# Float64 weights decoded by a shifted upper word plus a remainder, with the list of operations written anew, in a delta-rule and gated-MLP kernel

## The chip, the cores and the metric

One NeuronCore of one Trainium2 chip runs the whole program. The metric is the device time of one execution in microseconds (us); several runs are made and the median counts.

## What is computed

Four batches of eight heads run a delta rule over 768 steps with a 48 by 48 state, and the result `x` (4 x 768 x 384) goes through a gated MLP with a spatial gate:

```python
y[:, :, t] = einsum('bhd,bhde->bhe', q[:, :, t], state)
v_old = einsum('bhde,bhd->bhe', state, kt)              # kt: normalised key
state = state + bt * einsum('bhd,bhe->bhde', kt, vt - v_old)
...
h = maximum(x @ w_in, 0.0)                              # w_in 384 x 1024
u, v = h[..., :512], h[..., 512:]
v_n = (v - mean(v)) / sqrt(var(v) + 1e-06)
v_s = einsum('ts,bsd->btd', w_spatial, v_n) + b_spatial[None, :, None]
out = (u * v_s) @ w_out                                 # w_out 512 x 384
```

`w_in` and `w_out` are scaled by `1.0 / np.sqrt(...)` and so reach the kernel as float64; all else is float32. [...] 

## The kernel before

The recurrence is worked in chunks of 64 steps: 24 steps `s` (two halves of the batch, 12 chunks each), each for 16 batch-head pairs at once. Four steps form a group `g` (six groups). `prep(g)` loads `k`, forms the key products on TensorE (`kk`), copies them to a tile `xt` (L391), transposes the 32x32 blocks into `la` (L569, VectorE), normalises by the key lengths (L577 to L591), inverts the triangular blocks, and transposes the result back into `xt` (L638). Groups 0 and 1 have mode "w": there the inversion is 16 wide and runs on VectorE in PSUM (`lanes16`, L623 to L628), and `widen16` completes it with TensorE matmuls (tiles `bbc`, `gi`: L702, L718, L720). Groups 2 to 5 have mode "p": a 32-wide inversion on GpSimd (`lanes`, L608 and L613). After this `widen(s)` (tiles `tn`, `pi`), `kqt(s)` and `step(s)` carry the state from chunk to chunk.

Every second step gives a tile of 2 x 128 rows of `x` (`convert`, tiles `xh` and `xl`) to the MLP: `mlp_v` (matmuls with `win` as the 512-wide moving operand), `norm_v`, `mlp_u` (256 columns), and, when a batch half is complete, `gate` with the spatial matmuls (`wsph`, `wspl`) and the output (`wout`). The first MLP matmul needs all six tiles of `w_in` decoded; `weights()` decodes them, 128 x 512 each, and then four tiles of `w_out`, 128 x 384 each.

`load_f64` decodes one tile. With `w1` the upper and `w0` the lower word: L450 (VectorE) takes the exponent field out of `w1`; L452, L453 and L454 (ScalarE) clamp it and turn it into the exponent of a float32; L455 (ScalarE) turns `w0` into a fraction; L456 (VectorE) adds the sign; L458 (VectorE) and L459 (ScalarE) turn the mantissa bits of `w1` into a fraction; L460 adds the two fractions and L461 multiplies by the power of two (VectorE or GpSimd). `split_w` then rounds to the high part (L440, ScalarE) and subtracts for the low part (L441, VectorE or GpSimd). That is six steps on ScalarE, three on VectorE, and three that a table gives to VectorE or GpSimd.

What sets the order: `Plan.add` records every operation with its reads, writes and pools; `emit` then issues them in the order of a table of numbers, `ORDER` (two letters an operation), and a second table, `PICK`, names the engine where there is a choice. Each engine runs its instructions in that order and waits where an input isn't ready. The pair of letters that stands for no operation (`Qq`) makes `emit` put in a filler: two matmuls of 128 x 256 on the mask tile `mpos` into a free PSUM bank, whose result nobody reads. All loads and stores are issued from SyncE (L410), all matmuls from L517 (`mm`).

Of the kernel before, what the change touches and what calls it, by code (L numbers as in the profile page):

```python
# [32 lines left out]
NRAW = 7  # L33
NFULL = 6
# [8 lines left out]
    "2/1T132:2;2<Qq5g4f5i5n3p3q3y8x4N3r5j3u3v3$3!2>3(3%3#2?2@3&2[2]2^2_2{2|2}2~2,3031325l3s3x3c8l1U1f5o1s141g5m1G4Q5p5s1t"
    "5r5u1H4O4m333t4S4g34Qq354R364T3738391u3w3z4h3)3*4i5t4U5v4V4j4k1hQq1v3+4W2=3A4l5w5y5z5x5!5#5$5%5&3B5(3C3D3E3F3G424344"
    "3<454X4Z463-3.3/4Y4a4n4p3:4d4c4y4e4b4o5)4q3H4r4z3=4s4t4u4#3;1y3I4w5Q5*4x4$47491z4)1!Qq4(4*5+5-5.5/1#5:4!5;5<5=5>5?5@"
    "4&5[4%5]5^5_5{5K1$5L5|3>3?3@8m8n3[485}5~5,5M6o6p5V5N60614A8o5P621%5R4+631&6n645O3]6g6566673^4B5S6h5W685T4v5U1(Qq6i69"
    "1)8p8u4C6j4D6A4E8r6k6q6z6B6C6%6D1*8q6l5X5Y6r6m6E4F4G1+6FQq6&Qq6G4-6H5Z6s6!4H6t6#8s8t6u6x6y1-8v6v6w6I6J6K6L6M7i1.6N6O"
# [1068 lines left out]
```

## Time and profile before

| | us |
|---|---|
| median of 3 runs | 487.97 (487.59 to 488.6) |
| the profiled execution | 483.41 |
| its span in the trace | 481.7 |
| PE busy | 426.6 |
| DVE busy | 247.9 |
| ACT busy | 253.1 |
| POOL busy | 216.4 |

PE is TensorE's matmul stream, PEld its weight load, DVE VectorE, ACT ScalarE, POOL GpSimd, SP SyncE, which issues the DMAs. The span is the time from the first to the last recorded instruction, 1.7 us less than the profiled execution's own time. The profile comes from one execution, 4.6 us faster than the median. "issue" in the trace is time in which an engine waited for nothing that the profile shows. A tile's number is left out in the trace's names (`ut` for any of the six `ut` buffers), and a tile that lies in another's memory has that one's name (`wspl`, `xt` and `la` stand for different tensors early and late in the program).

### The profile page before, as it was taken

How to read it: one execution, taken by the hardware profiler on the slowest of the kernel's cores; microseconds unless marked ns; L12 is line 12 of the kernel's file. 1: busy time of each engine (PE TensorE's matmuls, PEld its weight loads, DVE VectorE, ACT ScalarE, POOL GpSimd, SP SyncE). 2: the span in 40 equal slices, each digit the busy share in tenths (PEclk: the TensorE clock that was granted, in tenths of full speed). 3: DMA queues.
4: the chain of work that ended last, by engine and by line, in shares of the span. 5: the costliest groups of instructions: out<-in, count | busy, mean ns of one | idle time of the engine just before them, and what ended most of it. 6: DMA issues, size and time to landing. Idle time of an engine off the chain costs nothing.

```text
span 481.7 us, 21693 instructions
## 1 busy us (share of the span) xinstructions
PE 426.6 (89%) x9722; PEld 380.7 (79%) x9722; DVE 247.9 (51%) x550; ACT 253.1 (53%) x592; POOL 216.4 (45%) x357
## 2 busy tenths in 40 slices
PE   2437888777989899998999999999899999999996
PEld 2336666665877787876988989999799899999996
DVE  2798895544765658846707345252645132441212
ACT  3788674346576869776227633415625484431113
POOL 3105547883489832389944668840001400122310
PEclk9555579885999999999999999999999999999999
DMA  8632153140425455452130341101420100001012
GB/s 266 250 99 81 58 155 103 50 141 4 150 60 178 135 170 198 135 151 86 57 106 6 99 137 36 56 1 35 145 81 14 59 0 18 1 1 49 3 65 99
DMA packets 26108, 42.65 MB, mean 89 GB/s; under 512 B 4512, under 2 KB 14880, under 8 KB 26016
## 3 DMA queue, kind: packets, MB, share of 16 engines
q1 hardware_dynamic: 26016, 41.27, 27.2%
q8 instruction: 76, 1.25, 1.1%
q14 instruction: 16, 0.13, 0.1%
HBM read 35.36 MB, written 4.72 MB: 83 GB/s over the span
## 4 chain that ended last, share of the span: by engine, by line
PE 78%; DVE 6%; issue 6%; ACT 6%; DMA 3%; SPq 1%; DVEq 0%; ACTq 0%
PE ps L517 78%; DMA ke<-in_k_t 2%; ACT xt L391 1%; DVE ps L626 1%; DVE prod L623 1%; SPq L410 1%; DMA bn<-in_bun 1%; ACT gt L890 1%; DVE pt L750 1%; ACT w L803 0%; ACT ut L453 0%; ACT ut L454 0%; ACT ut L452 0%; DVE wspl L587 0%; ACT vr L880 0%
## 5 line engine op out<-in xcount | busy, mean ns | idle before, releaser
L517 PE MATMUL ps<-wsph,vf 128*128 128x256 f32 x528 | 107.4, 286 | 0.0
L517 PEld LDWEIGHTS ps<-wsph,vf 128*128 128x128 f32 x528 | 86.7, 191 | 1.3
L613 POOL TENSOR_TENSOR wl<-wl,prod 128x60 f32<-128x60 f32 (+7 forms) x120 | 74.1, 617 | 9.3
L517 PE MATMUL ps<-wspl,vf 128*128 128x256 f32 x264 | 74.6, 283 | 0.0
L608 POOL TENSOR_TENSOR prod<-wl,la 128x60 f32<-128x60 f32 (+7 forms) x120 | 67.8, 565 | 10.2 <-DVE ps L626 1.1
L973 DVE TENSOR_TENSOR gt<-ps,bbc 128x512 f32<-128x512 f32 x24 | 16.6, 691 | 68.8 <-PE ps L517 68.7
L517 PEld LDWEIGHTS ps<-wspl,vf 128*128 128x128 f32 x264 | 50.4, 191 | 0.3
L517 PE MATMUL ps<-wout_h,g 128*128 128x384 f32 x128 | 35.3, 341 | 0.0
L994 ACT COPY ob<-ps 128x384 f32<-128x384 f32 x24 | 11.2, 479 | 42.6 <-PE ps L517 40.6
L391 ACT COPY xt<-xt 32x128 f32<-32x128 f32 (+1 forms) x91 | 31.7, 349 | 2.1
L391 ACT COPY xt<-ps 128x512 f32<-128x512 f32 (+1 forms) x37 | 17.7, 481 | 27.6 <-PE ps L517 27.6
L750 DVE TENSOR_TENSOR pt<-ps,mpos 128x512 f32<-128x512 f32 (+1 forms) x29 | 16.7, 593 | 28.7 <-PE ps L517 25.0
L517 PE MATMUL ps<-bn 64*64 64x64 f32 (+2 forms) x896 | 20.4, 241 | 11.1 <-DMA bn<-in_bun 5.0
L517 PEld LDWEIGHTS ps<-bn 64*64 64x64 f32 (+1 forms) x896 | 16.9, 145 | 15.3 <-issue 4.6
L517 PE MATMUL ps<-ke 64*64 64x64 f32 (+2 forms) x768 | 18.9, 257 | 9.0 <-issue 4.8
L517 PEld LDWEIGHTS ps<-ke 64*64 64x64 f32 (+1 forms) x768 | 16.0, 160 | 13.4 <-issue 7.6
L803 ACT COPY w<-ps 128x384 f32<-128x384 f32 x24 | 11.5, 477 | 27.0 <-PE ps L517 26.9
L732 POOL TENSOR_TENSOR bn<-bn,nn 128x384 f32<-128x384 f32 x11 | 9.1, 835 | 36.4 <-DVE nn L600 15.9
L938 ACT ACTIVATE ut<-ps 128x256 f32<-128x256 f32 x48 | 17.9, 383 | 12.5 <-PE ps L517 12.4
L517 PEld LDWEIGHTS ps<-wout_h,g 128*128 128x128 f32 x128 | 23.2, 188 | 0.7
L517 PE MATMUL ps<-wout_l,g 128*128 128x384 f32 x64 | 21.1, 337 | 0.0
L517 PE MATMUL ps<-s,bn 48*64 48x48 f32 x704 | 16.4, 231 | 4.9 <-issue 3.5
(211 smaller groups left out, 1061.8 us busy)
## 6 DMA issues: line engine op xcount, KB each, us to landing
bn<-in_bun SPq DMA_DIRECT2D x46, 256.0 KB, 3.4
bn<-in_bun SPq DMA_DIRECT2D x48, 192.0 KB, 3.2
ke<-in_k_t SPq DMA_DIRECT2D x22, 256.0 KB, 4.0
out<-ob SPq DMA_DIRECT2D x24, 192.0 KB, 2.0
vf<-in_w_in SPq DMA_DIRECT2D x6, 512.0 KB, 6.2
g<-in_w_sp SPq DMA_DIRECT2D x3, 768.0 KB, 4.4
g<-in_w_out SPq DMA_DIRECT2D x4, 384.0 KB, 4.1
xs<-xs SPq DMA_DIRECT2D x66, 16.0 KB, 2.7
```

Source lines behind the costliest of these rows:

```text
L391: (nc.scalar.copy if e == "ACT" else ENG[e].tensor_copy)(out=out_, in_=in_)
L410: return P.add("SP", 0.39 if k.get("kb") else 0.57, lambda: nc.sync.dma_start(out=out_() if callable(out_) else out_, in_=in_() if callabl ...
L517: nc.tensor.matmul(o, l, r, start=start, stop=stop)
L608: P.add("POOL", cost, lambda: nc.gpsimd.tensor_tensor(out=pt if j else dst, in0=w3[:, :n, j : j + 1].broadcast_to([128, n, m]), in1=la3[:, ...
L613: P.add("POOL", cost, lambda: nc.gpsimd.tensor_tensor(out=dst, in0=dst, in1=pt, op=ALU.add), rd=["prod"], wr=[kw], pr=p0 + 2)
L623: P.add("DVE", cost, lambda: nc.vector.tensor_tensor(out=pt(), in0=w4()[:, :, :n, j : j + 1].broadcast_to([128, 2, n, m]), in1=lj.unsqueez ...
L732: P.add("", {"DVE": 0.56, "POOL": 0.83}, fn=lambda e: ENG[e].tensor_tensor(out=v, in0=v, in1=n.unsqueeze(3).broadcast_to([128, 2, 4, HD]), ...
L750: nc.vector.tensor_tensor(out=pt.rearrange("p (d a c) -> p d a c", d=2, a=2)[:, d], in0=v.rearrange("p d (a c) -> p d a c", a=2), in1=mpos ...
L803: P.add("ACT", 0.48, lambda: nc.scalar.copy(out=v3(w, 192), in_=v3(pc, 512)[:, :, 0:192]), rd=["pc"], wr=[("w", s % 2)], pr=pr)
L938: nc.scalar.activation(out=dst[:, :, o * 128 : o * 128 + 128], in_=src[:, :, j], func=AF.Relu)
L973: P.add("DVE", 0.69, lambda: nc.vector.tensor_tensor(out=gt(), in0=v3(bank(h.unit), 256), in1=bbc[0][:, th * 256 : th * 256 + 256].unsquee ...
L994: P.add("ACT", 0.48, lambda: nc.scalar.copy(out=ob_[t.unit], in_=bank(h.unit)[:, :DM]), rd=[("po", b, th, o)], wr=[("ob", b, th, o)], pr=4 ...
```

## The change

`load_f64` decodes in another way, and does the split itself. The magnitude of the upper word (sign bit off: `Abs` on ScalarE or a bitwise AND on VectorE) is clamped as a float32, shifted left by three bits and given the top two bits of `w1` back: this is the weight's upper part as a float32 in the tile `e`. The power of two is masked out of it into `st`; the lower word times 2^-52 times that power is the remainder. The high part is `e` rounded, and the low part is `e` minus the high part plus the remainder. `cst` shrinks from six constants to three. `FULL` is new and False, so that the conditions it stands in choose as before. `ORDER` and `PICK` are replaced as a whole.

```diff
+FULL = False
...
 ORDER = (
-    "070506040A0D000102030B0E080G090H0I0C0J0]0^0K0Y0_0L0F1V1W2O3l0N0P0Q1I1i0M2P2M2l2m3m1X0R0{0S1w1a0T0U0V0W0X1J0Z1N0}0b0c"
...
+    "0407090605000102030J0Y080A0B0KQW0@0*0[QW0D0]0^0_0E0C0L0+0G0|0-0.0/0F0H0I0;1N0<1OQW1Y0N2U0M1P0P2R0:2S2V21221C2XQW2a0Q"
...
     def consts():
-        for i, x in enumerate((-896.0, 254.0, 254.0 * 2.0**23, 0.0, 1e-30, EPS)):
+        for i, x in enumerate((0.0, 1e-30, EPS)):
...
-    def load_f64(key, hi, lo, src, n, pr, spr, acq, raw, e, st):
+    def load_f64(key, hi, lo, src, n, pr, spr, acq, raw, e, st, rel):
...
+        def size(z):
+            if z == "ACT":
+                nc.scalar.activation(out=e(), in_=wf(), func=AF.Abs)
+            else:
+                nc.vector.tensor_scalar(out=eu(), in0=w1(), scalar1=0x7FFFFFFF, scalar2=None, op0=ALU.bitwise_and)
+
+        P.add("", {"ACT": a, "DVE": d}, size, rd=[key], wr=[ek], pr=pre(pr))
         P.add("DVE", d, lambda: nc.vector.tensor_scalar(
-            out=eu(), in0=w1(), scalar1=20, scalar2=0x7FF, op0=ALU.logical_shift_right, op1=ALU.bitwise_and), rd=[key], wr=[ek], pr=pre(pr), port=True)
-        P.add("ACT", a, lambda: nc.scalar.activation(out=e(), in_=eu(), func=AF.Relu, bias=cst[:, 0:1]), rd=["cst"], wr=[ek], pr=pr)
-        P.add("ACT", a, lambda: nc.scalar.activation(out=e(), in_=e(), func=AF.Relu, scale=-1.0, bias=cst[:, 1:2]), rd=["cst"], wr=[ek], pr=pr)
-        P.add("ACT", a, lambda: nc.scalar.activation(out=eu(), in_=e(), func=AF.Identity, scale=-(2.0**23), bias=cst[:, 2:3]), rd=["cst"], wr=[ek], pr=pr)
-        P.add("ACT", a, lambda: nc.scalar.activation(out=st(), in_=w0(), func=AF.Identity, scale=2.0**-52, bias=1.0), rd=[key], wr=[sk], pr=pr)
+            out=e(), in0=e(), scalar1=2.0**-15, scalar2=122879.9921875, op0=ALU.max, op1=ALU.min), wr=[ek], pr=pre(pr), port=True)
+        P.add("DVE", d, lambda: nc.vector.tensor_scalar(
+            out=eu(), in0=eu(), scalar1=3, scalar2=0x3FFFFFFF, op0=ALU.logical_shift_left, op1=ALU.bitwise_and), wr=[ek], pr=pre(pr), port=True)
         P.add("DVE", dve_t(n), lambda: nc.vector.scalar_tensor_tensor(
-            out=eu(), in0=w1(), scalar=0x80000000, in1=eu(), op0=ALU.bitwise_and, op1=ALU.bitwise_or), rd=[key], wr=[ek], pr=pre(pr), port=True)
-        P.add("DVE", d, lambda: nc.vector.tensor_scalar(out=w1(), in0=w1(), scalar1=0xFFFFF, scalar2=None, op0=ALU.bitwise_and), wr=[key], pr=pre(pr), port=True)
-        P.add("ACT", a, lambda: nc.scalar.activation(out=w1().bitcast(F32), in_=w1(), func=AF.Copy, scale=2.0**-20), wr=[key], pr=pr)
-        P.add("", both(n), fn=lambda z: ENG[z].tensor_add(out=st(), in0=st(), in1=w1().bitcast(F32)), rd=[key], wr=[sk], pr=pr)
-        P.add("", both(n), fn=lambda z: ENG[z].tensor_mul(out=st(), in0=st(), in1=e()), rd=[ek], wr=[sk], pr=pr)
+            out=eu(), in0=w1(), scalar=0xC0000000, in1=eu(), op0=ALU.bitwise_and, op1=ALU.bitwise_or), rd=[key], wr=[ek], pr=pre(pr), port=True)
+        P.add("ACT", a, lambda: nc.scalar.activation(out=wf(), in_=w0(), func=AF.Copy, scale=2.0**-52), wr=[key], pr=pr)
+        P.add("DVE", d, lambda: nc.vector.tensor_scalar(out=su(), in0=eu(), scalar1=0xFF800000, scalar2=None, op0=ALU.bitwise_and), rd=[ek], wr=[sk], pr=pre(pr), port=True)
+        P.add("ACT", act_t(n), lambda: nc.scalar.copy(out=hi, in_=e()), rd=[ek], wr=[(key, "h")], pr=pr)
+        P.add("", both(n), fn=lambda z: ENG[z].tensor_mul(out=st(), in0=st(), in1=wf()), rd=[key], wr=[sk], pr=pr, rel=rel[0])
+        P.add("", both(n), fn=lambda z: ENG[z].tensor_sub(out=e(), in0=e(), in1=hi), rd=[(key, "h")], wr=[ek], pr=pr)
+        P.add("", both(n), fn=lambda z: ENG[z].tensor_add(out=lo, in0=e(), in1=st()), rd=[ek, sk], wr=[(key, "l")], pr=pr, rel=rel[1])
```

In the changed file the steps of one tile stand on L455 (`Abs`) or L457 (AND), L460, L462, L464 and L467 (VectorE), L466 and L468 (ScalarE), and L469, L470, L471 (VectorE or GpSimd); matmuls are on L524 and DMAs on L411.

The new order is seen best on three engines. First ScalarE, from where the 16-wide inverse of group 0 has been copied out (`wl`) to the first copies of `gi` and `pi`, which TensorE waits for in the widening. Before (the copy to `wl` is three rows above the first one shown):

```order
L455 ACTIVATE ut_403<-vf_343 128x512
L391 COPY wspl<-ps 128x512
L454 ACTIVATE ut_403<-ut_403,cst 128x512
L718 ACTIVATE gi<-ps 128x128
L452 ACTIVATE ut_395<-ut_395,cst 128x512
L452 ACTIVATE ut_339<-ut_339,cst 128x512
L453 ACTIVATE ut_339<-ut_339,cst 128x512
L454 ACTIVATE ut_339<-ut_339,cst 128x512
L453 ACTIVATE ut_395<-ut_395,cst 128x512
L454 ACTIVATE ut_395<-ut_395,cst 128x512
L718 ACTIVATE gi<-ps 128x128
L693 ACTIVATE pi<-ps 128x256
```

Now:

```order
L642 COPY wl<-ps 128x2x16x16
L455 ACTIVATE ut_490<-vf_367 128x512
L392 COPY xt_492<-ps 128x512
L725 ACTIVATE gi<-ps 128x128
L392 COPY wspl<-wspl 32x16x32
L455 ACTIVATE g_461<-g_461 128x384
L392 COPY wspl<-wspl 32x16x32
L725 ACTIVATE gi<-ps 128x128
L392 COPY wspl<-wspl 32x16x32
L466 ACTIVATE vf_325<-vf_325 128x512
L392 COPY xt_492<-ps 128x256 x2
L700 ACTIVATE pi<-ps 128x256
```

Six decode steps stood between the two copies of `gi`; now one stands there, with two copies of group 1's tile (`wspl`; `xt_492` belongs to group 2).

Second TensorE, at the first MLP matmuls (`win_h,xh` and `xh,win_h`). Before:

```order
L517 MATMUL ps<-bn_73,xt_222 64x48 x16
L517 MATMUL ps<-mpos 128x256
L517 MATMUL ps<-win_h,xh 128x512 x2
L517 MATMUL ps<-xh,win_h 128x256 x3
L517 MATMUL ps<-xh,win_l 128x256 x3
L517 MATMUL ps<-xl,win_h 128x256 x3
L517 MATMUL ps<-win_h,xh 128x512 x2
L517 MATMUL ps<-xh,win_h 128x256 x3
L517 MATMUL ps<-w_75,bn_73 48x48 x16
L517 MATMUL ps<-pt_71,w_75 48x64 x16
```

Now:

```order
L524 MATMUL ps<-w_76,bn_74 48x48 x16
L524 MATMUL ps<-pt_72,w_76 48x64 x16
L524 MATMUL ps<-ke 64x64 x32
L524 MATMUL ps<-wspl,bbc 16x16 x32
L524 MATMUL ps<-gi,bbc 32x16 x32
L524 MATMUL ps<-bn_73 64x64 x16
L524 MATMUL ps<-xh,win_h 128x256 x3
L524 MATMUL ps<-xh,win_l 128x256 x3
L524 MATMUL ps<-xl,win_h 128x256 x3
L524 MATMUL ps<-win_h,xh 128x512 x2
```

The first MLP matmul was the 73rd row of TensorE's list and is now the 94th: the steps 2 and 3 of the recurrence (`w_75`, `w_76`) and the first widening matmuls of group 1 (`wspl,bbc`) stand ahead of it. Of the fillers (25, now 32) 4 stood ahead of the first MLP matmul and 23 do now; 21 stood behind it, and 9 do now.

Third GpSimd, from its first decode step. Before:

```order
L732 TENSOR_TENSOR bn_74<-bn_74,nn_95 128x384
L643 MEMSET wl 128x1024
L460 TENSOR_TENSOR ut_403<-ut_403,vf_343 128x512
L690 MEMSET xt_222 32x4x32 x4
L460 TENSOR_TENSOR ut_228<-ut_228,vf_226 128x512
L461 TENSOR_TENSOR ut_228<-ut_228 128x512
L732 TENSOR_TENSOR bn_73<-bn_73,nn_95 128x384
L690 MEMSET xt_222 32x4x32 x4
L441 TENSOR_TENSOR win_l<-ut_327,win_h 128x512
```

Now:

```order
L469 TENSOR_TENSOR ut_192<-ut_192,vf_188 128x512
L470 TENSOR_TENSOR ut_192<-ut_192,win_h 128x512
L739 TENSOR_TENSOR bn_73<-bn_73,nn_95 128x384
L471 TENSOR_TENSOR win_l<-ut_192 128x512
L469 TENSOR_TENSOR ut_234<-ut_234,vf_190 128x512
L470 TENSOR_TENSOR ut_234<-ut_234,win_h 128x512
L469 TENSOR_TENSOR ut_279<-ut_279,vf_276 128x512
L470 TENSOR_TENSOR ut_279<-ut_279,win_h 128x512
L471 TENSOR_TENSOR win_l<-ut_234 128x512
L739 TENSOR_TENSOR bn_74<-bn_74,nn_95 128x384
```

Of the eighteen steps that may run on either engine for `w_in`, GpSimd had 9 and has 16 now. As before, all of them stand ahead of the first `lanes` of group 2.
## Rows read from the trace of the kernel before

**Rows 1.** The page: busy time by engine, and the chain that ended last.

```profile
PE 426.6 (89%) x9722; PEld 380.7 (79%) x9722; DVE 247.9 (51%) x550; ACT 253.1 (53%) x592; POOL 216.4 (45%) x357
...
PE 78%; DVE 6%; issue 6%; ACT 6%; DMA 3%; SPq 1%; DVEq 0%; ACTq 0%
```

**Rows 2.** Busy time of each engine by stage, granted clock, DMA share and GB/s.

```profile
24.00:36.00 12.00, 4.13 (x326) 3.70 (x324) 10.96 (x28) 10.02 (x19) 1.09 (x1) 0.50 0.37 102
...
108.00:120.00 12.00, 8.98 (x264) 6.63 (x267) 5.37 (x18) 7.07 (x18) 4.28 (x11) 0.57 0.02 4
...
288.00:312.00 24.00, 24.00 (x250) 22.49 (x250) 9.80 (x12) 9.89 (x25) 20.24 (x25) 1.00 0.15 48
```

**Rows 3.** Timeline, 0 to 30 us: start, duration, engine, instruction, idle before and releaser.

```profile
7.26 1.07 ACT L391 COPY xt<-ps 128x512 f32<-128x512 f32 x2 [4.74 <-PE ps L517]
...
12.29 0.63 PE L517 MATMUL ps<-ke 64*32 64x32 f32 x34 [4.82 <-issue]
...
13.66 1.91 DVE L569 STREAM_TRANSPOSE la<-xt 128x1024 f32<-128x1024 f32 x1 [3.73 <-ACT xt L391]
...
18.77 0.19 DVE L628 SCALAR_TENSOR_TENSOR ps<-ps,la 128x30 f32<-128x30 f32 x1
...
27.94 2.08 DVE L638 STREAM_TRANSPOSE xt<-wl 128x1024 f32<-128x1024 f32 x1
```

**Rows 4.** Timeline, the first two copies of `gi` on ACT.

```profile
30.87 0.28 ACT L718 ACTIVATE gi<-ps 128x128 f32<-128x128 f32 x1
...
35.15 0.26 ACT L718 ACTIVATE gi<-ps 128x128 f32<-128x128 f32 x1
```

**Rows 5.** Groups by line, the decode of `w_in`: busy us, mean ns | idle before.

```profile
L453 ACT ACTIVATE ut<-ut,cst 128x512 f32<-128x512 f32 x6 | 4.3, 713 | 0.1
...
L455 ACT ACTIVATE ut<-vf 128x512 f32<-128x512 uint32 x6 | 3.7, 656 | 0.0
...
L440 ACT CAST win_h<-ut 128x512 fp32r<-128x512 f32 x6 | 3.6, 621 | 0.0
...
L450 DVE TENSOR_SCALAR ut<-vf 128x512 uint32<-128x512 uint32 x6 | 2.4, 419 | 5.4 <-DMA vf<-in_w_in 5.4
...
L456 DVE SCALAR_TENSOR_TENSOR ut<-vf,ut 128x512 uint32<-128x512 uint32 x6 | 4.0, 676 | 0.0
...
L441 POOL TENSOR_TENSOR win_l<-ut,win_h 128x512 fp32r<-128x512 f32 x4 | 5.5, 1380 | 7.2 <-issue 3.7 <-ACT win_h L440 3.5
```

**Rows 6.** Timeline: small steps on DVE without and beside a POOL step.

```profile
16.99 0.19 DVE L582 TENSOR_TENSOR t<-nl 128x32 f32<-128x32 f32 x1
...
53.81 0.76 DVE L582 TENSOR_TENSOR t<-nl 128x32 f32<-128x32 f32 x1
...
54.49 2.50 POOL L461 TENSOR_TENSOR ut<-ut 128x512 f32<-128x512 f32 x2
...
55.83 1.70 DVE L587 TENSOR_TENSOR wspl<-wspl,sq 128x512 f32<-128x512 f32 x1
...
56.94 1.72 POOL L441 TENSOR_TENSOR win_l<-ut,win_h 128x512 fp32r<-128x512 f32 x1
...
58.01 0.22 DVE L623 TENSOR_TENSOR prod<-ps,wspl 128x56 f32<-128x56 f32 x1
```

**Rows 7.** Timeline, 65 to 82 us: first MLP matmuls and group 1's inverse.

```profile
69.70 1.42 PE L517 MATMUL ps<-win_h,xh 128*128 128x512 f32 x2
...
72.43 0.63 PE L517 MATMUL ps<-win_h,xh 128*128 128x512 f32 x2
...
78.23 2.12 DVE L638 STREAM_TRANSPOSE wspl<-wspl 128x1024 f32<-128x1024 f32 x1
...
81.30 0.69 PE L517 MATMUL ps<-wspl,bbc 32*16 32x16 f32 x64
```

**Rows 8.** A filler behind the first MLP matmuls, in the timeline.

```profile
82.38 0.59 PE L517 MATMUL ps<-mpos 128*128 128x256 f32 x2
```

**Rows 9.** What PE waited for from 66 to 130 us: total us, times, longest.

```profile
PE ps L517 <- issue: 5.8, 4, 2.5
```

More of the change, by code (lines that the diff above doesn't have):

```diff
@@ L43 @@
[L43 to L47, printed above, removed]
@@ L86 @@
+    "11111100011000100000100010100110100100"
 )
@@ L290, in delta_rule_gated_mlp @@
     prod = new("prod", 256)
-    cst = new("cst", 6)
+    cst = new("cst", 3)
     tn, pi = new("tn", NS * 32), new("pi", NS * 32)
@@ L458, in load_f64 @@
[L458 to L461 removed]
+        ek, sk = (key, "e"), (key, "s")
@@ L475, in weights @@
             load_f64(key, win_h[:, cols], win_l[:, cols], w_in[k * 128 : k * 128 + 128, c * 512 : c * 512 + 512], 512, 900 + idx, 60 + idx,
-                     [("full", h1), ("u", h2)], t1, lambda t2=t2: t2()[:, 0:512], st)
-            P.ops[-2].rel = [("full", h1)]
-            split_w(st, (key, "s"), lambda cols=cols: win_h[:, cols], lambda cols=cols: win_l[:, cols], 512, 900 + idx, [("u", h2)])
-        P.add("X", 0.0, None, rd=[((("win", i), "s"), "l") for i in range(2 * NK)], wr=["win"])
+                     [("full", h1), ("u", h2)], t1, lambda t2=t2: t2()[:, 0:512], st, ([("full", h1)], [("u", h2)]))
+        P.add("X", 0.0, None, rd=[(("win", i), "l") for i in range(2 * NK)], wr=["win"])
         for idx in range(ND):
@@ L539, in kk @@
                     c = pj * 64
-                    for h in range(2 if g == 0 else 1):
+                    for h in range(2 if not FULL and g == 0 else 1):
                         for d, a in COMBOS:
                             k = ks(ke, 0, d, a, p, j, 64)
-                            if g:
+                            if g or FULL:
                                 mm(one(hold, d)[a * 64 : a * 64 + 64, c : c + 64], k, k)
@@ L548, in kk @@
                                 mm(one(hold, d)[half(a, j, 0), c : c + 64], k[:, half(0, j, 0)], k)
-            P.add("PE", 0.6, kk, kind="kk" if g else "kk2", rd=[kk_, "pz"], wr=bk + [("kk", s)] + [q for k in (range(s, s + GP) if s4 == 0 else (s,)) for q in xk(k)], pr=400 + s, acq=acq)
+            P.add("PE", 0.6, kk, kind="kk" if g or FULL else "kk2", rd=[kk_, "pz"], wr=bk + [("kk", s)] + [q for k in (range(s, s + GP) if s4 == 0 else (s,)) for q in xk(k)], pr=400 + s, acq=acq)
             def ev(e, s=s, h=h):
@@ L562, in prep @@
         xg = lambda: blocks(xt_of(g))
-        for a in range(2 if g else 0):
+        for a in range(2 if g or FULL else 0):
             for j in range(2):
@@ L595, in prep @@
         if mode == "w":
-            P.add("ACT", 0.59, lambda: nc.scalar.copy(out=bank(ph.unit), in_=cst[:, 3:4].broadcast_to([128, 512])), rd=["cst"], wr=["wp"], pr=p0 - 1, acq=[("pm", ph)])
+            P.add("ACT", 0.59, lambda: nc.scalar.copy(out=bank(ph.unit), in_=cst[:, 0:1].broadcast_to([128, 512])), rd=["cst"], wr=["wp"], pr=p0 - 1, acq=[("pm", ph)])
             P.add("ACT", 0.2, lambda: nc.scalar.copy(out=v3(bank(ph.unit), 256)[:, :, 0 : 15 * 17 + 1 : 17], in_=v3(dv, 16)), rd=["sq"], wr=["wp"], pr=p0)
```

98 lines of the change are left out of this document (50 added, 48 removed).

## The prediction, written before the changed kernel was run

> **What bounds the kernel now.** I read the page first. TensorE is busy for 426.6 of the 481.7 us of the span, and 78% of the chain that ended last are its matmuls [rows 1]; the other engines are busy about half the time. This is an average over two different stages, so the table by stage comes next [rows 2]. From 288 to 312 us PE is busy for 24.00 of 24.00 us at full clock: what ScalarE, VectorE or GpSimd save there is worth nothing. From 24 to 36 us PE is busy for 4.13 of 12 us at the half clock (0.50), while DVE has 10.96 and ACT 10.02: here the weights are decoded and the first two groups are inverted, and PE waits. Between the two lies a stage where PE has enough work and still loses time: 8.98 of 12 us from 108 to 120, at a mean clock of 0.57. The change can gain in the first stage and in the middle one, and in the last only by giving PE fewer matmuls.
>
> In the first stage the timeline shows one thread [rows 3]: the key products end late, because PE stood for 4.82 us on something that the profile doesn't name ("issue") until 12.29; the transpose to `la` starts at 13.66, the 16-wide inversion at 18.77 and the transpose back at 27.94, to 30.0. The same thread for group 1 ends with the transpose at 78.23 to 80.35, and PE starts group 1's widening at 81.30; the first MLP matmul was at 69.70 [rows 7]. The other losses of PE behind that are small and many: from 66 to 130 us the largest sum is "issue", 5.8 us in four places [rows 9].
>
> **The change part by part.** I make the sum against the profiled execution, 483.41 us, and carry it over to the median of 487.97.
>
> ScalarE loses three of six steps a tile. For `w_in` a tile cost three clamping steps at 0.71, two conversions at 0.66 and a rounding at 0.62 [rows 5]: 4.07 us, or 24.4 for six tiles. Now it is an `Abs` (five of six tiles) and a conversion, both priced at the 0.66 of L455, and the rounding: 5 x 0.66 + 6 x 0.66 + 6 x 0.62 = 11.0. So ACT gets 13.4 us back. Little of it is on the path. Where it is, is the widening of group 0: the first copy of `gi` ran at 30.87 and the second, with six decode steps between, at 35.15 [rows 4]. Now one decode step and two copies stand there, some 1.9 us in place of the 4.28. I take 2.0 us gained; the ends are 0 (PE's own "issue" gaps set the pace there) and 4.3 (all of the distance).
>
> VectorE had for `w_in` six each of 0.42, 0.68 and 0.42 us and nine two-input steps at 0.68: 15.2 us without disturbance, with L458 taken as its like L450 [rows 5]. Now there are six tiles of three one-input steps at 0.42 and one two-input step at 0.68, one more one-input step, and two two-input steps at 0.68: 13.4 us. The clamp (L460) and the shift (L462) don't occur before; their ends are L450's 0.42 and L456's 0.68, and I take 0.42, since like L450 they have one input; at the other end they cost 3.1 us more. That is 1.8 us less, and DVE is what the thread of group 1 waits for, so I count all of it. Against it stands the place: between the transpose to `la` and the inversion of group 0 there were L450 and the mask step, about 1.1 us, and there are now the four decode steps of one tile, 1.9 us: 0.8 us lost.
>
> GpSimd takes 16 of the 18 movable steps of `w_in` in place of 9, at 1.38 each [rows 5]: 9.7 us more. GpSimd's own inversion of group 2 starts only behind group 1's blocks, so by itself this is covered: POOL is busy for 1.09 of 12 us from 24 to 36 [rows 2]. Without the cover it would be late for group 2 by up to 9.7 us. What it does to DVE is the first rival.
>
> The cost of a POOL step beside DVE is seen in the trace [rows 6]: L582 takes 0.19 us alone and 0.76 beside a POOL step, and L587 takes 1.70 with two POOL steps running, while L623, which reads PSUM, takes 0.22 in the middle of a POOL step. So the inversions of the 16-wide groups are safe, and the decode steps and the small steps on SBUF are not. Before lost 0.57 us on the one and, with L456 as the like of L587, 1.0 on the other; I take the same 1.6 for the change, so no term of the sum, because most POOL steps of tiles 0 to 2 fall beside the inversion of group 0. The Trainium skill ("SBUF — State Buffer", section "SBUF: two separate sides") speaks against the change: whichever of GpSimd or a VectorE step in a two-port mode or with two SBUF inputs starts first holds the pair for the whole instruction, and the other is blocked. The trace agrees in kind (0.76 for 0.19); by that rule each decode step that meets a POOL step could lose up to that step's whole length.
>
> The new first rows of ACT hold a second table load, and the clearing of a PSUM bank now comes ahead of both. ACT stood idle for 4.74 us before its first copy of `xt` [rows 3], which covers a load and a copy; without that cover the copies of the first key products come later by some 2 us, and the third and fourth products, which end the stage, still come at 12.29 or later. So nothing.
>
> On SyncE's queue two loads of `w_in` now stand ahead of the key tiles of the third and fourth step. That could make their products late by the two loads; but before, these products waited for PE's unnamed gap until 12.29 anyway [rows 3], long after the tiles could be there. I cost it at nothing; if the gap went and the loads stayed, the products would come earlier, not later.
>
> The first MLP matmul moves behind the steps 2 and 3 and the start of group 1's widening. By 81.30 PE had done 13 MLP matmuls of 512 columns and 15 of 256. With 0.63 us for two of 512 [rows 7] and half of that a matmul for 256 these are 6.5 us; in exchange some 1.4 us of key products of group 2 have been done ahead. PE owes 5.0 us at that point.
>
> Behind that point 12 fillers of two matmuls fall away, at 0.59 each [rows 8]: 7.1 us. A filler in a gap cost nothing, so I take 60%, 4.3. With the owed MLP work at hand PE has something to run in the gaps from 82 to 120 us: of the 5.8 us of "issue" I take 3.0 back [rows 9]. A mean clock of 0.57 over 12 us means some 10 us at the lower level, 1.2 GHz [rows 2]; dense matmuls take up to twice as long there, so up to 5 us lie in it, and I take 1.5.
>
> The sum: -2.0 - 1.8 + 0.8 + 5.0 - 4.3 - 3.0 - 1.5 = **-6.8 us**: 476.6 for the profiled execution and 481.2 for the median. Its ends: 0 from ScalarE, no gap won back and no filler worth anything give 488 + 4.0 = 492; all of 4.3 from ScalarE, all 7.1 of the fillers, all 5.8 of "issue" and 3.0 from the clock give 488 - 16 = 472.
>
> **The rivals.**
> 1. GpSimd blocks VectorE (slower). Between the back transpose of group 0 and the inversion of group 1 DVE has 16 decode steps (twelve with one input, four with two), and POOL's steps of the last three tiles run at that time. If each waits for half a POOL step, 0.69, that is 11 us on the thread of group 1, and the time is 481.2 + 11 = 492. It decides from about 10 of the 16 on. For it: the rows on L582 and L587 [rows 6]. Against it: POOL's steps wait for ACT's conversions and roundings, so there aren't always any. By the skill's rule with a whole step each it would be 22 us; no row here shows so much at once.
> 2. PE runs dry ahead of group 1's widening (slower). Nothing of the MLP stands there now. If DVE ends group 1 no earlier than 80.35 as before [rows 7], nothing comes from ScalarE and VectorE, the 5.0 us owed are paid in full, the gaps aren't won back, and the fillers give some 3: 488 + 5 - 3 = 490. For it: in the first MLP rows PE now has no other work than that of group 1. Against it: the 23 fillers ahead of the MLP.
> 3. No difference: the gaps without a named cause ("issue") recur whatever the order, ScalarE's relief falls into its idle time, and fillers and debt cancel: 488.
> 4. A larger gain: fillers ahead of the MLP keep the clock up, all 12 fillers behind it are saved and the gaps close: -2.0 - 1.8 + 0.8 + 5.0 - 7.1 - 5.8 - 3.0 = -13.9, or 474.
>
> That the change doesn't do what it says can be left out: the order shows three ScalarE steps fewer a tile.
>
> **How the numbers follow.** The sum above gets 0.48, the larger gain 0.15, no difference 0.09, the blocked VectorE 0.15, the dry PE 0.13. A measurement of this kernel can tell about 0.2% (1 us) from no change. So faster 0.63, same 0.09, slower 0.28. The likeliest case lies from 476 to 486; the range over all cases that leaves out no more than 2 in 10 goes from 471 to 493.
>
> **What would show it.** Right: the second copy of `gi` within about 3 us of the first; group 1's back transpose at about 75 to 76 us; full clock and few "issue" waits from 80 to 120; ACT busy some 20 us less in all. Wrong: decode steps on DVE (L460, L462, L467) at well over 0.42 us between 30 and 60 (rival 1); a wait of PE of several us for the back transpose ahead of the first MLP matmul, with the clock at half (rival 2); the same clock and waits from 80 to 120 (rival 3).

## The result, and the profile after

The change took 473.46 us (median of 4 runs, 471.26 to 476.53) where the kernel before took 488.29 (median of 4 on the same chip): a ratio of 0.970, 95% interval 0.963 to 0.977, or 14.8 us less. The forecast was 481.2, 6.8 less than 487.97: the sign was right and the size less than half. The time of the fourth rival, 474, is what came. Some executions of a kernel take 1 to 2% longer than its others; the ratios leave these out and the medians do not, so that a median and its ratio need not agree. The profiled execution took 471.30 us with a span of 469.6; before had 483.41 and 481.7, so the two traces differ by 12.1 us, and these are what can be followed in rows.

The page of the change, busy time and the chain that ended last, against [rows 1]:

```profile
PE 427.7 (91%) x9736; PEld 379.4 (81%) x9736; DVE 248.5 (53%) x558; ACT 230.6 (49%) x546; POOL 236.4 (50%) x371
...
PE 81%; issue 5%; DVE 3%; ACT 3%; DMA 3%; SPq 2%; POOL 2%; ACTq 0%; DVEq 0%; POOLq 0%
```

ScalarE lost 22.5 us of work and GpSimd got 20.0 more. PE runs the same matmuls as before, and 14 more for fillers (9736 for 9722). The fillers take 24.8 us for 18.3, all other matmuls 402.9 for 408.3, and PE is idle for 41.9 us in place of 55.1.

The stages of [rows 2], now:

```profile
24.00:36.00 12.00, 8.05 (x328) 6.09 (x326) 10.89 (x28) 5.79 (x12) 8.48 (x8) 0.70 0.68 216
108.00:120.00 12.00, 10.51 (x284) 8.53 (x284) 7.09 (x26) 6.54 (x18) 1.95 (x6) 0.86 0.12 31
288.00:312.00 24.00, 24.00 (x559) 21.76 (x558) 8.02 (x17) 9.07 (x24) 19.73 (x27) 1.00 0.19 58
```

In the first row DVE is as full as before (10.89 for 10.96) although ACT fell from 10.02 to 5.79; of the 3.9 us that PE is busier there 3.1 are fillers. In the second the clock is 0.86 for 0.57.

The thread of the first two groups, in the timelines of the four engines (start, duration, engine, instruction), against [rows 3, 4, 7]:

```profile
13.64 1.95 DVE L576 STREAM_TRANSPOSE la<-xt 128x1024 f32<-128x1024 f32 x1 [1.26 <-ACT xt L392]
...
17.48 1.28 POOL L469 TENSOR_TENSOR ut<-ut,vf 128x512 f32<-128x512 f32 x1 [12.17 <-ACT vf L466]
...
17.63 1.18 DVE L589 TENSOR_TENSOR t<-nl 128x32 f32<-128x32 f32 x1
...
18.72 1.27 POOL L470 TENSOR_TENSOR ut<-ut,win_h 128x512 f32<-128x512 f32 x1
...
19.11 1.16 DVE L467 TENSOR_SCALAR ut<-ut 128x512 uint32<-128x512 uint32 x1
...
21.21 0.20 DVE L635 SCALAR_TENSOR_TENSOR ps<-ps,la 128x30 f32<-128x30 f32 x1
...
30.60 2.06 DVE L645 STREAM_TRANSPOSE xt<-wl 128x1024 f32<-128x1024 f32 x1
...
34.18 0.28 ACT L725 ACTIVATE gi<-ps 128x128 f32<-128x128 f32 x1 [2.85 <-PE ps L524]
...
36.31 0.28 ACT L725 ACTIVATE gi<-ps 128x128 f32<-128x128 f32 x1
...
77.33 2.11 DVE L645 STREAM_TRANSPOSE wspl<-wspl 128x1024 f32<-128x1024 f32 x1
...
81.00 0.47 PE L524 MATMUL ps<-wspl,bbc 32*16 32x16 f32 x38 [0.29 <-ACT xt L392]
...
85.52 1.01 PE L524 MATMUL ps<-xh,win_h 128*128 128x256 f32 x3
```

The first stage gained nothing. `la` starts at the same time as before, the inversion of group 0 begins 2.4 us later, its transpose back 2.7 later; group 1's transpose back is at 77.33 for 78.23 and PE begins its widening at 81.00 for 81.30. The first MLP matmul is at 85.52 for 69.70. Up to 90 us PE had begun 13 MLP matmuls (4 of 512 columns, 9 of 256) for 36 before (18 and 18), and 2272 small ones for 2197. At 0.118 us for 256 columns, the pace of PE from 400 to 440 us in the trace, the missing ones (14 of 512 and 9 of 256 columns) are 4.4 us; less the 75 small ones more, at 0.012 to 0.019 each (38 in 0.47 us above, 34 in 0.63 in [rows 3]), the change is an estimated 3 us behind at 90 us. All of its 12 us come after that.

Where they come from is seen in the windows. First PE's busy time in six stretches, before (the first numbers behind the comma are PE, and the clock is third from the end):

```profile
0.00:90.00 90.00, 56.96 (x2243) 47.45 (x2247) 63.53 (x145) 56.90 (x120) 39.20 (x80) 0.68 0.45 142
90.00:130.00 40.00, 33.54 (x1160) 26.96 (x1150) 23.61 (x53) 22.07 (x56) 23.90 (x42) 0.83 0.25 76
130.00:170.00 40.00, 36.83 (x1128) 29.68 (x1124) 25.72 (x61) 26.61 (x69) 34.98 (x58) 1.00 0.42 127
170.00:250.00 80.00, 75.05 (x1899) 64.04 (x1887) 47.39 (x108) 51.22 (x123) 46.52 (x76) 1.00 0.44 136
250.00:310.00 60.00, 58.59 (x1147) 54.19 (x1146) 26.08 (x43) 27.89 (x66) 40.87 (x65) 1.00 0.22 67
310.00:380.00 70.00, 67.60 (x1491) 62.21 (x1490) 33.20 (x83) 31.65 (x81) 18.01 (x29) 1.00 0.16 48
```

And of this the fillers alone (tile `mpos` on PE), before:

```profile
90.00:130.00 40.00, 3.26 (x9) 0.83 0.25 76
130.00:170.00 40.00, 3.40 (x12) 1.00 0.42 127
170.00:250.00 80.00, 6.14 (x20) 1.00 0.44 136
```

The same two views of the change:

```profile
0.00:90.00 90.00, 63.85 (x2331) 50.62 (x2332) 67.72 (x157) 45.81 (x100) 49.76 (x84) 0.74 0.45 142
90.00:130.00 40.00, 37.03 (x1293) 29.51 (x1295) 25.56 (x62) 23.58 (x59) 22.85 (x41) 0.95 0.31 91
130.00:170.00 40.00, 37.45 (x1157) 30.42 (x1147) 27.34 (x68) 26.16 (x70) 33.59 (x53) 1.00 0.52 162
170.00:250.00 80.00, 76.24 (x1768) 67.00 (x1768) 45.59 (x96) 46.76 (x107) 49.25 (x81) 0.98 0.39 117
250.00:310.00 60.00, 60.00 (x1184) 55.63 (x1183) 28.78 (x56) 26.66 (x68) 43.44 (x63) 1.00 0.18 51
310.00:380.00 70.00, 66.95 (x1385) 60.37 (x1384) 26.59 (x75) 34.36 (x86) 24.59 (x43) 1.00 0.22 64
```

```profile
90.00:130.00 40.00, 0.70 (x2) 0.95 0.31 91
130.00:170.00 40.00, 0.59 (x2) 1.00 0.52 162
170.00:250.00 80.00, 4.04 (x14) 0.98 0.39 117
```

Idle time and fillers together are the time in which PE does nothing useful; the sum can be compared between two kernels only where the clock is alike, since PE takes longer for the same matmuls at the lower clock (in [rows 7] two of 512 columns take 1.42 us at a clock of 0.50 and 0.63 at 1.00). From 90 to 130 us it is 40 - 33.54 + 3.26 = 9.7 us before and 40 - 37.03 + 0.70 = 3.7 now; then 6.6 and 3.1, 11.1 and 7.8, 1.4 and 0, 2.4 and 3.1. From 90 to 380 us the change has 13.5 us less of it: 6.1 up to 130, where the clock is also higher (0.95 for 0.83), and 7.5 from 130 to 380, where the clock is nearly the same. Of the 13.5, 7.5 are fillers (12.8 before, 5.3 now) and 6.1 idle time (18.4 and 12.3); of the idle time 3.5 lie ahead of 130 us and 2.6 behind. From 380 us to the end PE is idle for 3.7 and 3.4 us. So behind 90 us 13.7 us are won, and the matmuls that are not fillers take 1.6 us more (358.5 for 356.9): the owed work, less what the higher clock gives back. That makes the 12.1. How much the clock gives back, some 1.4 us if 3 were owed, follows by subtraction alone.

From 130 to 380 us it is PE's waits for other engines and for loads that fell, from 7.6 to 2.7 us; its waits without a named cause rose from 4.0 to 6.5.

### The profile page after: what moved, and what is told of

Its sections match the earlier page's. It is cut to its first block, busy times and chain, and to the rows that moved or that the text cites. A ratio compares the mean times of both kernels' runs of the same rounds, so it can differ in the third digit from the quotient of the medians.

```text
span 469.6 us, 21728 instructions
## 1 busy us (share of the span) xinstructions
PE 427.7 (91%) x9736; PEld 379.4 (81%) x9736; DVE 248.5 (53%) x558; ACT 230.6 (49%) x546; POOL 236.4 (50%) x371
## 4 chain that ended last, share of the span: by engine, by line
PE 81%; issue 5%; DVE 3%; ACT 3%; DMA 3%; SPq 2%; POOL 2%; ACTq 0%; DVEq 0%; POOLq 0%
PE ps L524 81%; SPq L411 2%; DMA bn<-in_k_t 2%; ACT xt L392 1%; DMA bn<-in_bun 1%; POOL ut L470 1%; POOL ut L469 1%; ACT w L810 1%; DVE la L576 0%; DVE xt L645 0%; DVE ut L464 0%; DMA xs<-xs 0%; DVE g L464 0%; ACT xs L841 0%; DVE pt L757 0%
## 5 line engine op out<-in xcount | busy, mean ns | idle before, releaser
L524 PE MATMUL ps<-wsph,vf 128*128 128x256 f32 x528 | 107.2, 285 | 0.0
L524 PEld LDWEIGHTS ps<-wsph,vf 128*128 128x128 f32 x528 | 86.6, 190 | 1.1
L620 POOL TENSOR_TENSOR wl<-wl,prod 128x60 f32<-128x60 f32 (+7 forms) x120 | 76.4, 636 | 9.1
L615 POOL TENSOR_TENSOR prod<-wl,la 128x60 f32<-128x60 f32 (+7 forms) x120 | 70.4, 586 | 9.3
L524 PE MATMUL ps<-wspl,vf 128*128 128x256 f32 x264 | 74.6, 283 | 0.0
L524 PEld LDWEIGHTS ps<-wspl,vf 128*128 128x128 f32 x264 | 50.3, 191 | 0.3
L524 PE MATMUL ps<-wout_h,g 128*128 128x384 f32 x128 | 35.2, 339 | 0.0
L392 ACT COPY xt<-xt 32x128 f32<-32x128 f32 (+1 forms) x85 | 29.3, 345 | 5.4 <-DVE xt L392 3.6
L524 PE MATMUL ps<-bn 64*64 64x64 f32 (+2 forms) x896 | 19.7, 232 | 9.7 <-DMA bn<-in_k_t 5.9
L983 POOL TENSOR_TENSOR gt<-gt,ut 128x512 f32<-128x512 f32 x11 | 15.1, 1372 | 25.4 <-DVE gt L980 25.3
L524 PEld LDWEIGHTS ps<-bn 64*64 64x64 f32 (+1 forms) x896 | 16.2, 139 | 13.4 <-issue 10.3
L524 PE MATMUL ps<-mpos 128*128 128x256 f32 x64 | 24.8, 508 | 1.2 <-ACT xs L841 1.0
L985 ACT CAST g<-gt 128x512 fp32r<-128x512 f32 x16 | 9.9, 621 | 31.8 <-DVE gt L983 20.4
L524 PE MATMUL ps<-ke 64*64 64x64 f32 (+2 forms) x768 | 18.4, 254 | 6.7 <-ACT wl L642 3.3
L985 ACT CAST xt<-gt 128x512 fp32r<-128x512 f32 x8 | 5.0, 620 | 39.5 <-POOL gt L983 22.9
L524 PEld LDWEIGHTS ps<-ke 64*64 64x64 f32 (+1 forms) x768 | 15.6, 158 | 10.2 <-issue 4.0
L524 PEld LDWEIGHTS ps<-wout_h,g 128*128 128x128 f32 x128 | 22.9, 188 | 0.3
L887 ACT ACTIVATE vr<-ps 128x512 f32<-128x512 f32 x22 | 13.1, 595 | 18.5 <-PE ps L524 18.3
L739 POOL TENSOR_TENSOR bn<-bn,nn 128x384 f32<-128x384 f32 x14 | 11.9, 854 | 20.0 <-DVE ps L633 5.1
```

Of the source, the lines that this page charges most:

```text
L392: (nc.scalar.copy if e == "ACT" else ENG[e].tensor_copy)(out=out_, in_=in_)
L524: nc.tensor.matmul(o, l, r, start=start, stop=stop)
L615: P.add("POOL", cost, lambda: nc.gpsimd.tensor_tensor(out=pt if j else dst, in0=w3[:, :n, j : j + 1].broadcast_to([128, n, m]), in1=la3[:, ...
L620: P.add("POOL", cost, lambda: nc.gpsimd.tensor_tensor(out=dst, in0=dst, in1=pt, op=ALU.add), rd=["prod"], wr=[kw], pr=p0 + 2)
L739: P.add("", {"DVE": 0.56, "POOL": 0.83}, fn=lambda e: ENG[e].tensor_tensor(out=v, in0=v, in1=n.unsqueeze(3).broadcast_to([128, 2, 4, HD]), ...
L887: P.add("ACT", 0.69, lambda: nc.scalar.activation(out=raw_(r), in_=bank(h.unit), func=AF.Relu, accum_out=st[:, j : j + 1]), rd=[("pv", i)] ...
```

## The experiments

Every ratio is against runs of the kernel before on the same chip (medians of 486.45 to 489.85 us), with its 95% interval. "The list" is the table of operations that sets the order of the work. Two orders are joined where both have done the same steps. At 450 entries both have done 4, but the order before has 17 MLP pieces done and the new one 8; at 925 and 900 entries both have done 11 steps and 88 pieces. The choice of engines and the fillers go with the list: of 224 operations outside the decode that can run on two engines 63 change engine with the new order, and 61 of these stand behind entry 450. So what is called the order here is the order with its choice of engines.

### The decode and the order apart

```diff
 load_f64 as in the change
-ORDER, PICK of the change
+ORDER, PICK of the kernel before, each new decode step in the place of an old one
```

> The new decode with the old order of operations: each new decode step stands in the place of an old one (Abs on ScalarE, clamp, shift and insertion of the sign where the old exponent was put together; conversion and rounding where the old mantissa was converted), fillers as before. Theory O (the order behind 81 us earns the gain; the decode as such earns little): 485 to 488 us, ScalarE 20 us less busy without use. Theory D (the relief of ScalarE and VectorE by the decode is what earns it): 472 to 477 us.

```diff
 load_f64 as before
-ORDER, PICK of the kernel before
+ORDER, PICK of the change, each old decode step in the place of a new one
```

> The old decode with the new order: the old steps stand in the places of the new ones, the three clamping steps on ScalarE in the places of the Abs, the clamp and the shift; fillers as in the change. Theory O: 472 to 478 us, although ScalarE has its 20 us back. Theory D: 483 us or more; if the order only works because ScalarE has room, the extra steps delay the widening of group 0 and the time is above 488 us.

Measured: 495.19 us, ratio 1.020 (1.015 to 1.026), and 492.54 us, 1.013 (1.008 to 1.018). Neither half gives the gain, and each half alone is slower than before. The first time lies in neither range. The second is far from theory O's, and lies where the last clause of theory D put it: the new order stands still behind ScalarE, which has the old clamping steps in the way. PE's waits from 30 to 110 us in it:

```profile
PE ps L517 <- ACT ut L455: 4.9, 1, 4.9
PE ps L517 <- ACT xs L834: 4.5, 1, 4.5
PE ps L517 <- ACT wspl L391: 4.5, 2, 4.0
...
PE ps L517 <- ACT gi L718: 4.3, 2, 2.4
```

That is 18 us. In the first run PE is busy for 44.9 of the first 81 us where before it was for 50.2. So the first 80 us of an order seem to fit one decode alone, and this pair of runs says nothing on what comes behind. The next four runs leave the first stage as it is in one of the kernels.

### Where the order earns it

```diff
-ORDER of the change
+the first 450 (900) entries of it; then, in the old order, all entries not yet done
```

> The new decode, the new order for the first 450 entries of the list (to about 90 us: four steps, all of the decode of w_in), then everything that is left in the old order. Theory L (the order behind 81 us earns the gain by itself): 484 to 489 us. Theory S (what is done before 81 us sets up the gain, and the old order could use it as well): 471 to 477 us. Theory X (an order fits only its own program, each seam costs): above 489 us.

> The same with the first 900 entries (to about 165 us: eleven steps and the decode of w_out) in the new order. At this point the change is some 8 to 9 us ahead of the kernel before in matmuls done. Theory L: 475 to 480 us (the later 3 us are missing). Theory S: 471 to 477 us. Theory X: above 485 us.

```diff
-ORDER of the kernel before, old decode
+the first 450 (925) entries of it; then, in the new order, all entries not yet done
```

> The old decode, the old order for the first 450 entries (to about 90 us: four steps, all of the decode of w_in), then everything that is left in the new order. Theory L: 473 to 479 us. Theory S: 484 to 489 us. Theory X: above 489 us.

> The same with the first 925 entries (eleven steps, to about 170 us) in the old order. Theory L: 482 to 486 us (only the later 3 to 4 us are won). Theory S: 484 to 489 us. Theory X: above 489 us.

Measured: 486.74 us, 0.996 (0.990 to 1.003); 478.09, 0.981 (0.976 to 0.987); 474.32, 0.972 (0.965 to 0.979); 482.29, 0.989 (0.982 to 0.995). All four lie in the ranges of theory L. The third is the telling one: it has the old decode and the old start, and its ratio can't be told from that of the change (0.970). With the new decode and the new start, and the old order behind, nothing is left: idle time and fillers from 130 to 380 us are 21.7 us, for 21.5 in the kernel before and 14.0 in the change. The gain belongs to the order behind about 90 us, with its choice of engines; these two were not taken apart. Cut at 165 to 170 us it divides, by the ratios, into about 9 us ahead of the cut and between 5 and 6 behind.

```diff
-the first 450 entries of the order before, then the new order
+the first 300 (to about 65 us, no MLP matmul yet), then the new order
```

> The old decode and the old order for the first 300 entries (to about 65 us, no MLP matmul yet), then the new order. Theory L (only what comes behind counts, and the old start is as good): 471 to 476 us, as with 450 entries. If the 28 MLP matmuls ahead of 81 us are worth their 5 us to the new order: 476 to 480 us, 3 or more above the run with 450 entries.

Measured: 474.23 us, 0.971 (0.964 to 0.978), again the gain of the change, with another start still. PE's windows in it:

```profile
90.00:130.00 40.00, 34.09 (x1201) 28.06 (x1204) 21.15 (x59) 20.49 (x51) 25.75 (x42) 0.91 0.32 95
130.00:170.00 40.00, 37.26 (x1225) 29.30 (x1216) 26.18 (x62) 27.50 (x74) 29.45 (x49) 1.00 0.47 142
170.00:250.00 80.00, 76.20 (x1800) 66.81 (x1799) 47.63 (x106) 51.80 (x121) 56.31 (x85) 1.00 0.44 133
250.00:310.00 60.00, 60.00 (x1153) 55.80 (x1156) 29.57 (x52) 26.94 (x68) 41.14 (x62) 1.00 0.18 56
310.00:380.00 70.00, 70.00 (x1576) 63.60 (x1566) 27.25 (x76) 34.11 (x84) 30.38 (x52) 1.00 0.23 67
```

With 0.70 and 4.63 us of fillers in the first and third window, the time without useful work is 6.6 us from 90 to 130 (before 9.7) and 11.2 from 130 to 380 (before 21.5); from 250 to 380 PE has no gap at all. So what is won from 130 to 380 us does not hang on the start of the change: it comes with another start and another decode too.

### The fillers

```diff
-    "0407090605000102030J0Y080A0B0KQW0@0*0[QW0D..."
+    "0407090605000102030J0Y080A0B0K0@0*0[0D..."
```

`QW` is the entry for a filler; all are taken out, in the other kernel likewise.

> The change without its 32 fillers (matmuls of the mask whose result nobody reads). If they keep the granted clock up (theory F), the clock from 84 to 120 us falls from 0.74 to 1.00 to about 0.5 to 0.6 as in the kernel before, and the time is 476 to 480 us. If they are only PE time in idle gaps (rival), 470 to 472 us, or down to 467 where some of the 24.8 us of fillers stood in the way.

> The kernel before without its 25 fillers, 21 of them behind the first MLP matmul. If those behind it cost what the forecast took (4.3 of 7.1 us) and do nothing for the clock: 483 to 485 us. If they cost nothing (they stand in gaps): 488 us. If the clock depends on them: 490 to 494 us, with the granted clock below 1.00 somewhere between 120 and 240 us.

Measured: 470.68 us, 0.968 (0.962 to 0.973), where the change has 0.970; and 485.13 us, 0.998 (0.994 to 1.002), where the kernel before had 486.45 on the same chip. The first is in the range of the rival, that fillers are only PE time in gaps. The second lies between the three cases, but its interval (down to 3 us less) leaves out the 4.3 us that the forecast took. No worth of the fillers can be measured in either kernel. Two windows of the kernel before without them:

```profile
90.00:130.00 40.00, 33.64 (x1043) 28.25 (x1046) 23.67 (x54) 20.97 (x52) 26.32 (x47) 0.70 0.30 90
...
170.00:250.00 80.00, 67.67 (x1764) 57.91 (x1762) 46.38 (x104) 48.48 (x117) 43.68 (x71) 0.96 0.39 124
```

From 170 to 250 us PE is idle for 12.3 us, where with fillers it was idle for 5.0 and had 6.1 of fillers: the wait is about the same. The clock was lower in this execution, 0.70 for 0.83 in the first window and 0.96 for 1.00 in the second, and the time did not follow. That the missing fillers lowered it is not shown: over all executions the mean clock is 0.935 without them and 0.948 with them in the kernel before, but 0.954 without and 0.936 with them in the change.

### The MLP pieces between the small blocks

Until 112 us (before: until 116) the only MLP pieces that PE runs are the 22 of the first pair of steps. In the kernel before they are used up at 100.8 us, and from 102 to 115 us PE has only trains of small matmuls and fillers. Four runs move these pieces.

```diff
 order of the change
-the 22 pieces between the blocks of group 1's widening, to about 112 us
+the 22 pieces in one block ahead of it
```

> The change, with the same 22 pieces in one block ahead of group 1's widening (about 80 us) instead of between its blocks. Theory P: the trains of small matmuls from 95 to 115 us are bare again, with issue waits and the clock near 0.6 there: 476 to 481 us. Theory T: 471 to 475 us as in the change.

Measured: 480.26 us, 0.980 (0.975 to 0.984), in the range of theory P. By the ratios (0.980 and 0.970) that is about 5 us more than the change, with an uncertainty of 4; the two were not run beside each other. The windows and the wait for issue from 84 to 140 us:

```profile
100.00:120.00 20.00, 14.78 (x605) 12.57 (x597) 10.79 (x27) 8.35 (x22) 11.69 (x21) 0.50 0.21 60
...
PE ps L524 <- issue: 5.9, 5, 2.4
```

The same rows of the change:

```profile
100.00:120.00 20.00, 17.49 (x646) 14.38 (x646) 11.34 (x33) 12.35 (x34) 9.08 (x17) 0.91 0.23 66
...
PE ps L524 <- issue: 1.6, 3, 1.2
```

With bare trains the waits without a named cause are back (5.9 for 1.6; before had 6.0), and the clock is at the lower level of 1.2 GHz (0.50) for the whole window, in this one execution.

```diff
 order of the kernel before
-the 22 pieces from 69.7 us on
+one behind each small block from 81 to 112 us (spread), or all in one block at 81 us (late)
```

> The kernel before, with one thing moved: the 22 pieces of the first pair's MLP (18 matmuls of 512 columns, 36 of 256), of which 13 and 15 matmuls stood ahead of 81 us, are held back and stand one behind each small block of group 1's widening and of step 4, to about 112 us. Theory P (MLP pieces between blocks of small matmuls take away the issue waits and hold the clock): the waits for issue of 6.0 us from 84 to 140 us fall to about 2, the clock from 100 to 120 rises from 0.74 to about 0.9, and after the debt of 3 to 5 us the time is 480 to 485 us. Theory T (when the steps and the widening themselves run sets the end, pieces between them don't): the debt alone is seen, 489 to 494 us.

> The same 22 pieces held back to the same place, but in one block at about 81 us instead of spread. Theory P: the debt is paid and the bare trains of small matmuls from 90 on lose as before: 490 to 494 us. Theory T: the same 489 to 494 us as the spread one. If work held back to 81 us is enough, wherever it stands: 480 to 485 us.

Measured: 494.33 us, 1.006 (1.002 to 1.011), and 494.14 us, 1.011 (1.007 to 1.016). By the ratios, 3 and 5 us are lost. For the spread pieces that is what theory T said, and against theory P; the late block both theories put at 490 to 494, and it decides nothing between them. The windows of the spread kernel, in an execution of 495.58 us:

```profile
100.00:120.00 20.00, 17.35 (x585) 12.86 (x583) 6.64 (x19) 8.94 (x27) 10.79 (x21) 1.00 0.20 59
120.00:140.00 20.00, 18.50 (x371) 14.30 (x371) 12.82 (x27) 11.09 (x25) 6.36 (x14) 0.83 0.31 93
```

What theory P said of the stretch happened: from 100 to 120 us PE is busy for 17.35 us for 14.74, at full clock, and from 84 to 140 it waits 0.4 us for issue. The time went up all the same: by 130 us only 76 MLP matmuls and 3136 small ones were begun, for 99 and 3264 before, and this has to be paid behind.

```diff
 order of the kernel before
-the last 6 of the 22 pieces, from 91 to 100 us
+between the key products, steps and widenings from 102 to 115 us
```

> The kernel before; the last six MLP pieces of the first pair (18 matmuls of 256 columns) stand 25 to 100 places later in the list, between the key products, steps and widenings that ran bare from 102 to 115 us. Nothing else is moved, and no work is held back past that stretch. Theory P (pieces between the small blocks save issue waits and the clock): issue waits of 6.0 us from 66 to 140 fall below 4, the time is 483 to 487 us where before has 488 to 489. Theory T (the places of the steps and widenings decide; pieces only fill): 488 to 491 us, since the gaps where the pieces stood before are now empty.

Measured: 488.71 us, 1.001 (0.997 to 1.006), and PE's wait for issue from 66 to 140 us is as long as ever:

```profile
PE ps L517 <- issue: 6.1, 6, 2.0
```

So the place of these pieces is worth about 5 us within the new order, and no gain came from the three ways of moving them in the old one. What is left as the cause is the new order as a whole, pieces, steps and widenings with their engines. Which of its other moves does most was not found, and stays open.

### GpSimd beside VectorE

```diff
 PICK of the change
-16 of the 18 movable steps of w_in on POOL
+all 18 on DVE
```

> The change with the 16 movable steps of w_in that GpSimd does put on VectorE, in the same places. If GpSimd beside VectorE costs the thread of the first two groups (the forecast's first rival): VectorE's steps at 1.06 to 1.63 us instead of 0.42 to 0.7 go, and the time is 468 to 472 us. If the thread suffers more from 16 steps of 0.68 us on VectorE (11 us) than from the contention: 476 to 482 us. If the first stage has slack that the rest eats: 472 to 475 us.

Measured: 476.92 us, 0.976 (0.969 to 0.983): not told apart from the change. VectorE's timeline in it:

```profile
17.89 0.19 DVE L589 TENSOR_TENSOR t<-nl 128x32 f32<-128x32 f32 x1
...
19.67 0.20 DVE L635 SCALAR_TENSOR_TENSOR ps<-ps,la 128x30 f32<-128x30 f32 x1
...
79.03 2.11 DVE L645 STREAM_TRANSPOSE wspl<-wspl 128x1024 f32<-128x1024 f32 x1
```

The step that took 1.18 us beside L469 on GpSimd takes 0.19, and group 0's inversion starts 1.5 us earlier. Group 1's transpose back is 1.7 us later, since VectorE now has the 16 steps itself. Contention and work change places.

## Why the prediction was right and wrong

**What bounds the kernel** was read right in its first part (PE waits on the thread of groups 0 and 1) and cut too short in the second. The sum took gaps from 82 to 120 us alone, because the sample at 288 to 312 us is full [rows 2] and stood for all that comes behind. But from 130 to 380 us there were 11.9 us of idle time and 9.5 of fillers. **This is the step that failed:** the two terms for the gaps and the fillers, -3.0 and -4.3, stand for what the traces show as 13.5 us. The idle time fell by 6.1, of which 2.6 from 130 to 380 us, where the sum put it at nothing; and the 7.5 us of fillers that went came back as useful work in full, not to 60%.

That the miss is no larger is in part luck: the operations were to give 3.0 us and gave none to the end, and the debt was some 2 us smaller than taken. By the two traces the change is 12.1 us faster, by the medians 14.8; the 2.7 us between them are scatter of the executions and stand for no term.

**The gaps** from 90 to 130 us gave 3.5 us of idle time for the 3.0 taken, and **the clock** rose there, if not to full (0.95 for 0.83). That the owed MLP work is what PE runs in these gaps was right too: put in one block, it leaves them empty and costs about 5 us.

**The fillers.** "I take 60%, 4.3" was wrong in kind: a filler stands where PE would wait. Taken out, they gave -0.2% (-0.6 to +0.2). So what the fewer fillers of the change are worth is what stands in their place, and this is useful work: they belong in the gaps, by their full length, and not in a term of their own.

**The debt** of 5.0 us was right in kind and some 2 us too large: at 90 us 23 MLP matmuls fewer, against 75 small ones more, an estimated 3 us. It was paid.

**ScalarE, -2.0.** The copies of `gi` are 2.1 us apart for 4.3, as forecast, and ACT is busy for 22.5 us less; but the second copy comes at 36.31 for 35.15, because the first waits for a transpose that is 2.7 us later. **VectorE, -1.8 and +0.8.** Undisturbed, the clamp took 0.38, the shift 0.43, the two-input step 0.63 and the step that masks out the power of two (L467) 0.43, near what was taken; but beside GpSimd L589 took 1.18 and L467 1.16, 1.7 us on the thread of group 0 alone where the sum took 1.6 for both groups, and in group 1 L460 took 1.06, L464 1.63 and L587 0.86. The three terms promised 3.0 us and gave 0.9 at group 1's transpose (77.33, not 75 to 76). And they were worth nothing to the end: with the old decode and the old start the new order takes the same time.

**The rivals.** The first was seen in kind and stayed small. By the Trainium skill ("SBUF — State Buffer", section "SBUF: two separate sides") a GpSimd step that starts first keeps out, for its whole length, a VectorE step with two SBUF inputs or in a two-port mode. The trace agrees for L589, which has two SBUF inputs, began 0.15 us behind the POOL step L469 and ended 0.05 us behind its end. So does the 0.76 us of L582 in [rows 6]; the POOL step that it met is not shown there:

```profile
53.26 1.27 POOL L441 TENSOR_TENSOR win_l<-ut,win_h 128x512 fp32r<-128x512 f32 x1 [3.71 <-issue]
```

It ends at 54.53, and L582 at 54.57. But only five of VectorE's steps on the thread met one, some 4 us in all and not the 11 of the rival. The second came in part: PE did wait ahead of group 1, for a load of `bn`, 2.6 us, but made up for it. The fourth gave the time that was measured. Its two large terms, 7.1 for all the fillers and 5.8 for the gaps, are near the 7.5 and 6.1 of the traces; but 2.6 us of the gaps lie behind the stretch that it named, the operations' 3.0 us did not come, and its reason, that the fillers ahead of the MLP keep the clock up, is not borne out: without any filler the change is as fast (0.968). That the sum comes out at 474 is in part luck. Its 0.15 was too little because the case "the new order is denser as a whole" was priced by one stretch.

## What to carry to other kernels

When a table of numbers replaces the order of the whole program, add up idle time and fillers of the bounding engine over all stages, not only where the clock is low: a stretch at full clock with 2 to 8% of idle time is long, and its sum can be larger than that of the visible gap (here 21.5 us with the fillers, against 9.7). A change of operations that comes with a new order is best judged by joining the two orders at points where both have done the same steps; here the gain came without the new operations, on which the forecast spent most of its steps. Filler work is to be counted as waiting time, and such sums are to be compared at a like clock.

## What was not expected of the hardware

**The waits without a named cause stand at fixed places.** When the PE matmul records of a trace are counted from its start, the "issue" waits of the kernel before end at numbers 223, 605, 733, 860, 987, 1115, 1243, 1625 and so on: all 17 of them, 22.1 us, lie within two records of a grid of one in 127.5. So do the 19 of the change (15.3 us), and in the 16 traces no unnamed wait over 0.15 us is farther than 3 records from such a grid. Not every place has a wait. In the kernel before, of the 12 places where the 127 matmuls ahead had taken less than 3 us, 11 have one, 18.8 us together; of the 43 where they had taken more than 4.1 us, none has. This fits the runs on the MLP pieces: small matmuls alone reach the next place soon, and with matmuls of 256 and 512 columns among them the waits from 84 to 140 us are 0.4 and 1.6 us for 6.0. What is done at these places no run shows. The third rival's "recur whatever the order" was half right: the places are fixed, the waits are not.

**A lower clock need not cost time where PE waits.** In the profiled executions of the kernel before, with and without fillers, the mean clock is 0.925 and 0.897. Without fillers the matmuls that are not fillers take 13.6 us more (421.9 for 408.3), idle time and fillers together are 14.1 us less (59.3 for 73.4), and the spans are 481.7 and 481.2. In the kernel with the old start to 450 entries, an execution at a mean clock of 0.909 took 473.61 us and one at 0.970 took 475.02. That the lower clock is hidden where PE waits for others would explain both; it was not tested by itself. It is no rule for all kernels: with the 16 steps on VectorE, executions at 0.955 and 0.956 took 474.65 and 471.97 us, and those at 0.939 to 0.943 took 476.64 to 478.69.
